# A gated-MLP kernel with a hand-written planner: own PSUM tiles for the block products of v, measured durations in the planner, and another order of its steps

## The chip, the cores and the metric

The kernel runs on one core of one Trainium2 chip. The metric is the device time of one execution in microseconds (us), the median of several runs. The engines are named as in the profile: PE (TensorE, matmuls), DVE (VectorE), ACT (ScalarE), POOL (GpSimd) and SP (the sync engine, which here issues the DMAs).

## What is computed

Two parts follow one another: a block attention whose blocks are 64 tokens long, and a gated MLP on its result with a spatial mixing by `w_sg`. All of it is float32.

```python
def _attn_ref(q, k, v):                       # (batch, heads, seq, head_dim) = (8, 8, 576, 64), chunk = 64
    ...
    scores = scale * np.matmul(q_c, k_c.transpose(0, 1, 2, 4, 3))      # within each chunk of 64 tokens
    attn = np.exp(scores - np.max(scores, axis=-1, keepdims=True))
    attn = attn / (np.sum(attn, axis=-1, keepdims=True) + 1e-09)
    return np.matmul(attn, v_c).reshape(B, H, S, D)

def _moe_ref(x, w_in, g_ln, w_sg, b_sg, w_out):   # x (8, 576, 512), w_in (512, 1024), w_out (512, 512)
    h = gelu_tanh(x @ w_in)
    u, v = h[..., :512], h[..., 512:]
    v_n = (v - mean(v)) / np.sqrt(var(v) + 1e-06) * g_ln
    v_s = np.einsum('ts,bsd->btd', w_sg, v_n) + b_sg[None, :, None]
    return x + (u * v_s) @ w_out
```

## The kernel before

The work is cut by batch entry ("block" b, 0 to 7). Each block passes four stages: v (the right half of `x @ w_in`, then gelu and the layer norm), u (the left half), s (the mixing by `w_sg`, times u) and o (`@ w_out`, plus x, and the stores). Attention runs in tiles of 128 tokens: scores (S, 64x64 matmuls and a softmax), a transpose (T) and the product with the attention's values (O, 64x64 matmuls, copied out of PSUM into `xh`, `xl`, `xf`). The attention of a later block is laid between the MLP steps of an earlier one.

Every float32 operand is split into a high and a low part (`split`), and a product takes three matmuls (low by high, high by low, high by high). From block `FAST` = 2 on, the products of v, u and o are done by a seven-product scheme for 2x2 blocks: `product` (L1209) with number 1 to 7. Sums of weight blocks that it needs are made once by `w_sums` on POOL, kept in DRAM and loaded into the tile `wx` ahead of each stage (`next_extra`); sums of x blocks are made for each block by `x_sums` on POOL and split by ACT and DVE into `tx`.

PSUM is one pool of four tiles of two banks each (`ps_m`, `[P, 2, 512]` float32, program name `pm` in the trace). `v_fast` takes one such tile for two accumulators, `o["a"]` in the first bank and `o["b"]` in the second: product 1 into a, a copied out by ACT, product 5 into b, b copied out by ACT, product 6 into a, a copied out, product 3 into b, b added up by DVE, product 7 into a, and so on. A further tile `c` is taken in its last step. `u_fast`, by contrast, takes a tile of its own for each of its accumulators a, b and c, with both banks of each in use.

The order of all instructions is made when the program is built. Each call of an engine is recorded (`Recorder`, `Plan.add`) with its dependencies; `cells` and `masks` say which part of a tile an operand covers, for PSUM by the bank (2048 bytes). `Op.price` gives each instruction a duration and a lag, `Plan.due` a due time, and `Plan.run` simulates the engines and picks for each the ready instruction with the earliest due time. PE goes through its instructions in the order of the program but may look up to `AHEAD` = 10 us of work further. `EARLY` moves the due times of named steps, `LATE` = 60 ns is added to every wait between engines. `emit` (L230) then issues all instructions in the order of the simulated start times (L253, the one line that nearly all rows of the trace carry), and the framework below adds the semaphores, from the order in which it sees the instructions. Each engine executes its queue strictly in that order, so an instruction at the head that is not ready holds up all behind it.

The order that the planner starts from is written by hand. `START` (L48) lists the steps of blocks 0 and 1, the weight conversion and the first attention tiles: L and W, w (load, begin, end of the v half of `w_in`), X and x (the u half), Y (`w_out`), G and g (`w_sg`), A and B (loads of q/k and of the attention's values), S, T, O, P, Q (attention), v, u, s, o with block and step, V and Z (`w_sums` of u and of v), E (`odd_diff`) and J (`x_sums`). SP issues the loads of START in exactly this order up to the step `V0`. Blocks 2 to 7 run in the loop at its end; `SLOTS` says behind which unit of a block which attention steps are put (one list for odd blocks, one for even ones), and `SUMS` behind which units of block 2 the `w_sums` of o are put.

Of the kernel before, what the change touches and what calls it, by code (L numbers as in the profile page):

```python
# [25 lines left out]
P = 128  # L26
# [22 lines left out]
A0 L0 B0 A1 L1 L2 L3 B1 A2 A3 S0 W0 T0 S1 W1 S2 w0 w1 T1 W2 O0 O1 W3 w2 T2 S3 M0 w3 v00 O2 A4 T3 X0 O3 G0 S4 v01 A8 T4  # L49
O4 B8 x0 X1 v02 X2 x1 v03 X3 U1 v04 U0 x2 g0 g1 x3 g2 g3 P5 g4 F0 u02 u03 s00 T5 F1 T6 P7 s01 s02 Q5 T7 T8 s03 Q7 v10  # L50
v11 Y0 v12 v13 Y4 Y2 Y1 Y3 u10 u11 s10 u13 Y5 s11 Y6 Y7 u12 A10 V0 P9 B10 A11 V1 s12 o01 V2 S13 A12 T9 T10 o02 V3 P11 A15 T13 o03 s13 o00 Q9 B11 T11 T12 O13 B12 Z0 Z1 o10 Z2 o11 Z3 Q11 B15 P14 A17
E2 o12 o13 J0 J1 J2
"""

SUMS = {8: "o0", 9: "o1", 10: "o2", 11: "o3"}
# [12 lines left out]
    1: "0:T0 1:S4 1:T1 3:S23 4:T4 8:O01 8:T2 9:O4 10:T3 11:O23 11:S56",  # L68
    0: "0:T5 1:T6 2:S78 9:O56 9:T7 10:T8 12:O78 12:S9A",
# [7 lines left out]
FAST = 2  # L77
ORDER = "u0 u1 u2 u3 u4 s0 s1 s2 s3 o0 o1 o2 o3"
# [9 lines left out]
EARLY = {'K*': 0, 'X*': -8, 's03': 1, 'Y0': -2, 'P7': 3, 'v04': -4, 'X0': -1, 'w3': -1, 'W*': -1, 'g4': 5, 'Y7': -2}  # L88
# [4 lines left out]
LATE, DMA_LATE = 60, 3000  # L93
# [15 lines left out]
@functools.cache  # L109
def masks(ap, offset, width, psum):  # L110
    (step, n), *free = ap
    row, at = offset // step, offset % step
    idx = np.array([at])
    for st, c in free:
        idx = (idx[:, None] + st * np.arange(c)[None, :]).ravel()
    unit = 2048 if psum else 128 if step * width > 256 else 4
    mask = 0
    for i in np.unique(idx * width // unit):
        mask |= 1 << int(i)
    if psum:  # L120
        return (mask, 0, 0, 0)
    return tuple(mask if row < 32 * (q + 1) and row + n > 32 * q else 0 for q in range(4))
# [10 lines left out]
class Op:  # L133
# [11 lines left out]
    def price(self):  # L145

        n = max(a.free_size() for a in self.outs[:1] + self.ins[:2])
        psum = any(a.space == PSUM for a in self.outs + self.ins)
        if self.engine == "tensor":
            x = self.ins[-1]  # L150
            n = self.outs[0].free_size()
            if x.dtype == F32R:
                return (5.9 if n < 400 else 4.6) + 0.447 * n, 160
            if x.dtype == BF16:
                return 4.6 + 0.42 * n, 160
            if self.ins[0].ap[0][1] == D:
                self.quarter = True
                return 34, 160
            return (118 if self.method == "transpose" else 1.83 * n + 10), 160
        if self.method == "dma_start" and self.engine == "gpsimd":  # L160
            return 1200, DMA_LATE + self.ins[0].size() / 100
        if self.engine == "sync":
            row = self.ins[0].ap[-1][1]
            return (420 if row >= P else 620), DMA_LATE + self.ins[0].size() / row / 16 * (9 + 0.16 * row)
        wide = [a for a in self.ins if a.free_size() > 1]
        copies = self.method in ("tensor_copy", "tensor_scalar") and n > 1
        if self.engine == "gpsimd":
            self.waits = self.method == "tensor_tensor"
            self.locks = self.waits and n > 8
        if self.engine == "vector":  # L170
            if self.method == "memset":
                return 600, 80
            self.locks = self.waits = not psum and (len(wide) > 1 or copies)
            one = len(self.ins) == 1 and not psum and self.method in ("tensor_copy", "tensor_scalar")
            return 75 + (0.53 if one else 1.04) * n, 80
        if self.engine == "scalar":
            return 100 + 0.82 * n + (100 if len(self.outs) > 1 else 0), 100
        return (600 if "pow" in str(self.kwargs.get("op")) else 200 + 1.8 * n), 42
# [10 lines left out]
class Plan:  # L189
# [84 lines left out]
    def run(self, users, after, at):  # L274
# [41 lines left out]
        for _ in range(len(ops)):  # L316
# [39 lines left out]
            if e == "tensor" and op.quarter != mode:  # L356
                mode = op.quarter
                cost += 150
            if e == "scalar" and op.table not in (0, table):
                table = op.table  # L360
                cost += 1200
# [53 lines left out]
def block_attention_gated_mlp(ctx: ExitStack, tc: tile.TileContext, qkv, w_in, w_out, w_sg, g_ln, b_sg, out):  # L415
# [177 lines left out]
    def w_sums(kind, step):  # L593
# [5 lines left out]
        def whole(i, j):  # L599
            r = new()  # L600
# [7 lines left out]
        def store(n):  # L608
            before, nc.early = nc.early, 1000 * EARLY.get("K*", 0)
            for a, c in zip(kept[kind], extras()):  # L610
                nc.sync.dma_start(out=blocks_of(a, 3)[:, n].bitcast(F32), in_=c[:, n].bitcast(F32))
            nc.early = before

        if step == 0:
            kept[kind] = [spare.tile([P, 3 * 4 * P], F32R, name=f"kept_{kind}_{i}") for i in range(2)]
            sums["11"], sums["21"] = whole(0, 0), whole(1, 0)
            s3 = new()
            pick("c").tensor_tensor(s3, sums["11"], sums["21"], op=ALU.subtract)
            split_to([a[:, 1] for a in extras()], s3)
            store(1)  # L620
        elif step == 1:
            r = whole(1, 1)
            pick("c").tensor_tensor(sums["21"], sums["21"], r, op=ALU.add)
            pick("c").tensor_tensor(sums["11"], sums["21"], sums["11"], op=ALU.subtract)
            split_to([a[:, 0] for a in extras()], sums["11"])
            store(0)
        elif step == 2:
            r = whole(0, 1)
            pick("c").tensor_tensor(r, r, sums["11"], op=ALU.subtract)
            split_to([a[:, 2] for a in extras()], r)  # L630
            store(2)
        else:
            split_to(block(1, 0), sums["21"])

    wx, kept = {}, {}
    NEXT = {"v": "u", "u": "o", "o": "v"}

    def next_extra(kind, b, n):

        kind = NEXT[kind]  # L640
        if (b == FAST and kind == "o") or (b == B - 1 and kind == "v"):
            return
# [220 lines left out]
    def keep_tile(place, src):  # L863
        (b, c), (b1, c1) = place
        if b == b1 and c and (c != 4 or b < FAST):
# [31 lines left out]
    def keep(b, c, src, tiles=0):  # L897
# [21 lines left out]
        if c > 4 and b >= FAST:  # L919
# [69 lines left out]
    def v_unit(b, m):  # L989
# [7 lines left out]
        for kt in range(KT):  # L997
            ab = [(h_in, l_in)[k][:, kt, tok] for k in (1, 0, 0)]
            cs = win_h, win_l, win_h
            if b < FAST or kt < 2:  # L1000
# [421 lines left out]
```

## Time and profile before

| | before |
|---|---|
| median of 3 runs | 527.72 us (526.66 to 528.29) |
| the profiled execution | 529.48 us, of which the span from first to last instruction is 527.7 us |
| busy: PE, DVE, ACT, POOL | 483.1, 419.2, 346.2, 139.4 us |
| mean granted TensorE clock | 0.987 |
| blocks 0 and 1 with all preparation | until about 172 us |
| blocks 2 to 7 | about 58 to 65 us each, the last one without attention beside it |

The table of stages and the groups of instructions show where PE is idle and what ended the idle time; the timelines show the instructions of one engine in order, with the idle time before an instruction and its releaser in square brackets. In the names, `pm<-wx,tx` is a matmul that reads `wx` and `tx` and writes a PSUM tile. In stage v the names stand as `wx,tx`, `win_l,tx`, `wx,xh` (256 columns), in stage u as `tx,wx`, `tx,win_l` (288 columns), in stage o as `gl,wout` and the like.

### The profile page before, as it was taken

What the parts mean: (1) busy time and instruction counts of PE and PEld (TensorE: products, weight loads), DVE (VectorE), ACT (ScalarE), POOL (GpSimd) and SP (SyncE); (2) the same over time, 40 slices, a digit from 0 to 9 for tenths busy, and PEclk for the clock granted to TensorE, in tenths of its full rate; (3) what the DMA queues carried; (4) which work ended last, traced back from release to release, by engine and by line L of the source; (5) the groups of instructions that cost most, each with busy time, mean ns of one, the idle gap of its engine ahead of it and who ended that gap; (6) DMA issues with size and microseconds to landing.
All of it is one profiled execution on the core that took longest, in us unless ns stands there. A gap on an engine that the chain in (4) does not pass through costs nothing.

```text
span 527.7 us, 13136 instructions
## 1 busy us (share of the span) xinstructions
PE 483.1 (92%) x5305; PEld 449.5 (85%) x5310; DVE 419.2 (79%) x741; ACT 346.2 (66%) x629; POOL 139.4 (26%) x129
## 2 busy tenths in 40 slices
PE   3999999999978989999898899989997898998995
PEld 2568997999867988999898899989897888998995
DVE  7979998998947896897969696979757599685565
ACT  4887899436664897658973798549884398534420
POOL 0113100830354728133311421151301522130100
PEclk9999999999989999999999999999997999999998
DMA  8884102038627812487544643288520745055303
GB/s 331 289 240 132 41 1 81 1 107 240 219 69 231 260 52 87 138 264 234 164 114 135 193 165 101 87 233 256 162 97 5 233 133 141 20 155 176 121 0 91
DMA packets 80828, 76.53 MB, mean 145 GB/s; under 512 B 47100, under 2 KB 60672, under 8 KB 80768
## 3 DMA queue, kind: packets, MB, share of 16 engines
q1 hardware_dynamic: 80768, 75.69, 46.6%
q8 instruction: 42, 0.69, 0.5%
q14 instruction: 18, 0.15, 0.1%
HBM read 61.51 MB, written 14.16 MB: 143 GB/s over the span
## 4 chain that ended last, share of the span: by engine, by line
PE 31%; DVE 29%; ACT 22%; DMA 6%; issue 5%; POOL 4%; SPq 1%; DVEq 0%; POOLq 0%; ACTq 0%
PE pm L253 31%; ACT ptT L253 6%; DVE nmax L253 4%; DVE u L253 4%; DVE sm L253 3%; ACT u L253 2%; DVE xl L253 2%; DVE gl L253 2%; DMA out_dram<-ot 2%; DVE pt L253 2%; ACT L253 2%; ACT xf L253 2%; DVE st L253 2%; DVE wout L253 2%; DVE v L253 2%
## 5 line engine op out<-in xcount | busy, mean ns | idle before, releaser
L253 PE MATMUL pm<-wsg,v 128*128 128x288 f32 x768 | 109.3, 298 | 3.0 <-DVE ut L253 2.9
L253 PEld LDWEIGHTS pm<-wsg,v 128*128 128x128 f32 x768 | 103.7, 189 | 4.5 <-PE pm L253 2.2
L253 ACT COPY ptT<-blocks 32x256 f32<-32x256 f32 (+1 forms) x140 | 62.5, 447 | 12.5 <-DVE blocks L253 10.1
L253 POOL TENSOR_TENSOR sm<-sm,neg_half 128x1 f32<-128x1 f32 x36 | 30.1, 838 | 122.3 <-DVE sm L253 110.8
L253 PE MATMUL pm<-gh,wout 128*128 128x288 f32 x272 | 56.0, 303 | 2.1 <-DVE xl L253 1.1
L253 DVE TENSOR_TENSOR u<-pm,u 128x576 f32<-128x576 f32 (+1 forms) x50 | 36.0, 726 | 25.8 <-PE pm L253 25.2
L253 PEld LDWEIGHTS pm<-gh,wout 128*128 128x128 f32 x272 | 43.6, 192 | 3.5 <-issue 1.3
L253 POOL TENSOR_TENSOR pt<-pt,nmax 128x512 f32<-128x512 f32 x27 | 30.4, 1140 | 50.5 <-DVE nmax L253 44.9
L253 PE MATMUL pm<-gl,wout 128*128 128x288 f32 x136 | 36.4, 306 | 5.6 <-DVE gl L253 5.5
L253 ACT ACT_TABLE_LOAD x30 | 38.5, 1283 | 4.5 <-DVE pt L253 3.3
L253 ACT CAST gh<-u 128x576 fp32r<-128x576 f32 x32 | 21.4, 671 | 25.2 <-DVE u L253 25.1
L253 POOL TENSOR_TENSOR xs<-xf 128x576 f32<-128x576 f32 x12 | 18.2, 1513 | 60.8 <-ACT xf L253 41.1
L253 POOL TENSOR_TENSOR xs<-xf,xs 128x576 f32<-128x576 f32 x12 | 19.0, 1582 | 51.4 <-DVE tx L253 36.0
L253 DVE TENSOR_TENSOR gl<-u,gh 128x576 fp32r<-128x576 f32 x32 | 26.5, 833 | 6.5 <-ACT gh L253 6.1
L253 ACT CAST tx<-xs 128x576 fp32r<-128x576 f32 x24 | 16.1, 674 | 21.8 <-POOL xs L253 15.2
L253 PEld LDWEIGHTS pm<-gl,wout 128*128 128x128 f32 x136 | 24.3, 192 | 6.9 <-DVE gl L253 6.9
L253 DVE TENSOR_TENSOR ot<-pm,xf 128x576 f32<-128x576 f32 x32 | 23.8, 750 | 7.0 <-PE pm L253 4.9
L253 DVE TENSOR_TENSOR tx<-xs,tx 128x576 fp32r<-128x576 f32 x24 | 20.6, 865 | 10.9 <-ACT tx L253 10.7
L253 PE MATMUL pm<-xh,win_l 128*128 128x288 f32 x112 | 28.3, 299 | 0.0
L253 PE MATMUL pm<-qk 64*64 64x64 f32 x992 | 20.8, 228 | 8.0 <-DMA qk<-qkv 6.9
L253 PE MATMUL pm<-xh,win_h 128*128 128x288 f32 x112 | 28.0, 296 | 0.0
L253 PE MATMUL pm<-xl,win_h 128*128 128x288 f32 x112 | 28.0, 296 | 0.0
(185 smaller groups left out, 1329.4 us busy)
## 6 DMA issues: line engine op xcount, KB each, us to landing
qk<-qkv SPq DMA_DIRECT2D x31, 512.0 KB, 4.8
wx<-kept_u SPq DMA_DIRECT2D x36, 256.0 KB, 3.3
out_dram<-ot SPq DMA_DIRECT2D x31, 256.0 KB, 4.0
wx<-kept_v SPq DMA_DIRECT2D x30, 256.0 KB, 4.5
wx<-kept_o SPq DMA_DIRECT2D x30, 256.0 KB, 3.3
av<-qkv SPq DMA_DIRECT2D x116, 64.0 KB, 2.6
wsg<-w_in SPq DMA_DIRECT2D x4, 512.0 KB, 8.8
wout<-w_in SPq DMA_DIRECT2D x4, 512.0 KB, 6.8
```

What stands on the lines that cost most here:

```text
L253: getattr(getattr(self.nc, op.engine), op.method)(*op.args, **op.kwargs)
```

## The change

Each accumulator of `v_fast` gets a PSUM tile of its own. For the planner, a PSUM tile is now one cell, whichever bank is used. `Op.price` is rewritten with other durations and lags for nearly every kind of instruction, `LATE` goes from 60 to 0, and the change of PE between 64-row and 128-row matmuls costs 90 or 253 ns in the simulation where it cost 150. `START` is reordered, `SLOTS` has a list for each block, `SUMS` moves two of the sums of o, and `EARLY` grows from 11 to 71 entries. The sums of v's weights (`w_sums("v", ...)`) are computed in three steps in place of four, with block sums computed again where they were held before: 13 additions or subtractions on POOL where there were 8. The last store of the program is one addition over both halves, with two DMAs (one from SP, one from ACT's queue) where there were two additions and four DMAs from SP. `FAST_V` equals `FAST`, so that every test with it gives what it gave.

```diff
 START = """
-A0 L0 B0 A1 L1 L2 L3 B1 A2 A3 S0 W0 T0 S1 W1 S2 w0 w1 T1 W2 O0 O1 W3 w2 T2 S3 M0 w3 v00 O2 A4 T3 X0 O3 G0 S4 v01 A8 T4
...
-v11 Y0 v12 v13 Y4 Y2 Y1 Y3 u10 u11 s10 u13 Y5 s11 Y6 Y7 u12 A10 V0 P9 B10 A11 V1 s12 o01 V2 S13 A12 T9 T10 o02 V3 P11 A15 T13 o03 s13 o00 Q9 B11 T11 T12 O13 B12 Z0 Z1 o10 Z2 o11 Z3 Q11 B15 P14 A17
-E2 o12 o13 J0 J1 J2
+L0 A1 S0 L2 L1 A0 S1 L3 B1 A2 W3 W1 A3 T0 S2 W2 B0 T1 W0 w0 O1 A4 w2 X0 O0 T2 M0 w1 S3 w3 v00 O2 T3 S4 G0 O3 v01 T4
...
+Q7 v10 v12 v11 Y0 Y1 Y3 v13 Y5 u10 Y7 u11 Y2 Y6 s10 A11 u12 u13 s11 V0 P9 V1 T9 S13 s12 B10 A10 o01 V2 T10 o02 A12
+P11 T13 o03 s13 o00 V3 Q9 T11 B11 Z0 T12 O13 B15 Z1 o10 A17 o11 A15 B12 Z2 o13 Q11 E2 o12 J0 J2 P14 J1
 """
-SUMS = {8: "o0", 9: "o1", 10: "o2", 11: "o3"}
+SUMS = {(2, 8): "o0", (2, 9): "o1 o2", (2, 11): "o3"}
 SLOTS = {
-    1: "0:T0 1:S4 1:T1 3:S23 4:T4 8:O01 8:T2 9:O4 10:T3 11:O23 11:S56",
-    0: "0:T5 1:T6 2:S78 9:O56 9:T7 10:T8 12:O78 12:S9A",
+    2: "10:S9A 0:T5 10:O56 10:T8 12:O78 1:S78 4:T6 8:T7",
+    3: "9:T4 2:T1 2:S4 10:O4 1:T0 12:O23 3:S23 9:O01 8:T2 9:T3 9:S56",
+    4: "10:S9A 10:O56 8:T7 9:T8 2:T6 2:S78 1:T5 12:O78",
+    5: "9:T4 2:T1 10:O4 1:T0 3:S23 9:O01 2:S4 12:O23 8:T2 9:T3 9:S56",
+    6: "12:S9A 2:S78 8:T8 12:O78 10:O56 0:T5 6:T7 1:T6",
 }
-LATE, DMA_LATE = 60, 3000
+LATE, DMA_LATE = 0, 3000
@@ masks
-    unit = 2048 if psum else 128 if step * width > 256 else 4
+    if psum:
+        return (1, 0, 0, 0)
+    unit = 128 if step * width > 256 else 4
@@ Op.price (PE; GpSimd; ScalarE)
-                return (5.9 if n < 400 else 4.6) + 0.447 * n, 160
+                return 2.5 + 0.45 * n, 190
...
-        return (600 if "pow" in str(self.kwargs.get("op")) else 200 + 1.8 * n), 42
+            if "pow" in str(self.kwargs.get("op")):
+                return 870, 42
+            return (300 + 0.5 * n if not self.waits else 100 + (1.76 if self.kwargs["op"] == ALU.mult else 2.27) * n), 42
...
-            return 100 + 0.82 * n + (100 if len(self.outs) > 1 else 0), 100
+        slow = 120 * (len(outs) > 1) + 90 * (len(ins) > 1)
+        return (80 if psum else 100) + (0.8 if psum else 0.825) * n + max(slow, 105 * part), 100
@@ w_sums, kind "v" (new)
+            if step == 0:
+                r, r2 = whole(0, 0), whole(1, 0)
+                add(r, r2, ALU.subtract)
+                keep_sum(1, r, r2)
+            elif step == 1:
+                r, r2 = whole(1, 0), whole(1, 1)
+                add(r, r2)
+                whole(0, 0, r2)
+                add(r, r2, ALU.subtract)
+                whole(0, 1, r2)
+                add(r2, r, ALU.subtract)
+                keep_sum(0, r)
+                keep_sum(2, r2)
+            else:
+                r, r2 = whole(1, 0), whole(1, 1)
+                add(r, r2)
+                split_to(block(1, 0), r)
@@ v_fast
-            ab = ps_m.tile([P, 2, 512], F32, name="pm")
-            o["a"], o["b"] = ab[:, 0], ab[:, 1]
+            o["a"], o["b"] = (ps_m.tile([P, 2, 512], F32, name="pm")[:, 0] for _ in range(2))
@@ o_fast, the last step of block 7
-            for e in range(2):
-                es = slice(e, e + 1)
-                o_part(d, ot, ot, es)
-                o_store(b, 1, 0, ot, es)
+            o_store(b, 1, 0, o_part(d, ot, ot), last=nc.scalar)
```

## Rows read from the trace of the kernel before

**Rows 1.** The page, part 1: busy time, share of the span, instructions by engine.
```profile
PE 483.1 (92%) x5305; PEld 449.5 (85%) x5310; DVE 419.2 (79%) x741; ACT 346.2 (66%) x629; POOL 139.4 (26%) x129
```
**Rows 2.** Busy time by stretch: length, engines' busy (x instructions), granted clock, DMA share, GB/s.
```profile
0.00:40.00 40.00, 29.49 (x361) 20.07 (x364) 33.41 (x72) 28.63 (x63) 4.58 (x10) 1.00 0.84 288
40.00:140.00 100.00, 98.88 (x1041) 91.21 (x1042) 92.90 (x179) 69.94 (x127) 25.08 (x22) 1.00 0.33 97
140.00:172.00 32.00, 26.21 (x352) 23.29 (x351) 21.41 (x34) 18.45 (x45) 14.83 (x13) 0.95 0.55 161
```
**Rows 3.** PE groups of stage v: xcount | busy us, mean ns | idle before, releasers.
```profile
L253 PE MATMUL pm<-wx,tx 128*128 128x256 f32 x144 | 21.4, 289 | 4.7 <-ACT u L253 2.7 <-DVE u L253 2.0
L253 PE MATMUL pm<-win_l,tx 128*128 128x256 f32 x48 | 14.0, 291 | 1.8 <-ACT u L253 1.4 <-DVE u L253 0.5
L253 PE MATMUL pm<-wx,xh 128*128 128x256 f32 x48 | 10.4, 289 | 1.5 <-ACT u L253 1.5
```
**Rows 4.** Timeline of PE in stage v of block 7: start, duration, [idle before <-releaser].
```profile
474.12 0.52 PE L253 MATMUL pm<-wx,tx 128*128 128x256 f32 x3
475.31 1.35 PE L253 MATMUL pm<-wx,tx 128*128 128x256 f32 x9 [0.68 <-ACT u L253]
```
**Rows 5.** Timeline of ACT in the same stretch.
```profile
474.67 0.58 ACT L253 COPY u<-pm 128x512 f32<-128x512 f32 x1 [2.55 <-PE pm L253]
```
**Rows 6.** PE groups of stage u, columns as in rows 3.
```profile
L253 PE MATMUL pm<-tx,wx 128*128 128x288 f32 x144 | 21.7, 298 | 2.0 <-ACT ut L253 2.0
...
L253 PE MATMUL pm<-tx,win_l 128*128 128x288 f32 x48 | 14.7, 306 | 0.9 <-DVE ut L253 0.9
```
**Rows 7.** Timeline of PE where block 5 goes from s to o.
```profile
393.24 0.70 PE L253 MATMUL pm<-wsg,z 128*128 128x288 f32 x4
...
402.46 0.61 PE L253 MATMUL pm<-gl,wout 128*128 128x288 f32 x1 [0.88 <-DVE gl L253]
```
**Rows 8.** Timeline of DVE there.
```profile
396.35 1.21 DVE L253 TENSOR_REDUCE nmax<-pm 128x16 f32<-128x1024 f32 x1
...
398.57 0.75 DVE L253 TENSOR_TENSOR u<-pm,u 128x576 f32<-128x576 f32 x1
```
**Rows 9.** Two stretches at the lower clock, and block 5 from s to o; columns as rows 2.
```profile
148.97:152.38 3.41, 3.41 (x23) 2.76 (x22) 1.60 (x4) 1.78 (x5) 0.00 (x0) 0.50 0.09 20
401.55:408.38 6.83, 5.95 (x25) 5.92 (x25) 4.86 (x8) 3.17 (x5) 0.00 (x0) 0.50 0.00 0
390.00:416.00 26.00, 22.85 (x141) 21.39 (x141) 20.65 (x33) 10.83 (x20) 5.58 (x5) 0.87 0.39 128
```
**Rows 10.** PE waiting for gl in stage o: the group (as rows 3).
```profile
L253 PE MATMUL pm<-gl,wout 128*128 128x288 f32 x136 | 36.4, 306 | 5.6 <-DVE gl L253 5.5
```
**Rows 11.** Timeline of PE at the end of blocks 0 and 1.
```profile
148.76 0.70 PE L253 MATMUL pm<-gl,wout 128*128 128x288 f32 x2 [2.07 <-DVE gl L253]
...
157.01 0.51 PE L253 MATMUL pm<-qk 64*64 64x64 f32 x19 [1.17 <-ACT xf_lows L253]
```
**Rows 12.** Groups of ACT and POOL with durations that the planner prices.
```profile
L253 ACT COPY ptT<-blocks 32x256 f32<-32x256 f32 x112 | 45.2, 404 | 2.1
...
L253 POOL TENSOR_TENSOR sm<-sm,neg_half 128x1 f32<-128x1 f32 x36 | 30.1, 838 | 122.3 <-DVE sm L253 110.8 <-ACT z L253 6.2 <-DMA av<-qkv 3.3
...
L253 POOL TENSOR_TENSOR r<-win_h,win_l 128x512 f32<-128x512 f32 x8 | 10.7, 1337 | 2.8 <-DVE wx L253 1.5 <-DVE v L253 1.0 <-ACT ptT L253 0.3
```
**Rows 13.** Timeline of POOL: the first sum of x for block 2.
```profile
170.29 1.43 POOL L253 TENSOR_TENSOR xs<-xf 128x576 f32<-128x576 f32 x1 [5.62 <-DVE x_diff L253]
```
**Rows 14.** Timeline of PE and ACT at the start: the first scores, the first weight.
```profile
4.31 1.13 PE L253 MATMUL pm<-qk 64*64 64x64 f32 x32 [4.31 <-DMA qk<-qkv]
...
5.53 0.66 ACT L253 ACTIVATE wsg<-wsg 128x512 f32<-128x512 f32 x1 [2.80 <-DMA wsg<-w_in]
```
**Rows 15.** Timeline at the end: the last additions (DVE), the last store's issue (SP).
```profile
522.89 0.82 DVE L253 TENSOR_TENSOR ot<-pm,ot 128x288 f32<-128x288 f32 x2
...
524.74 0.42 SPq L253 DMA_DIRECT2D out_dram<-ot  x1
```

More of the change, by code (lines that the diff above doesn't have):

```diff
@@ L77 @@
 FAST = 2
+FAST_V = 2
 ORDER = "u0 u1 u2 u3 u4 s0 s1 s2 s3 o0 o1 o2 o3"
@@ L606, in split_to, with store, keep_sum @@
             split(place[0], place[1], src, nc.scalar, nc.vector)
-        def store(n):
+        def store(n, place):
             before, nc.early = nc.early, 1000 * EARLY.get("K*", 0)
-            for a, c in zip(kept[kind], extras()):
-                nc.sync.dma_start(out=blocks_of(a, 3)[:, n].bitcast(F32), in_=c[:, n].bitcast(F32))
+            for a, c in zip(kept[kind], place):
+                nc.sync.dma_start(out=blocks_of(a, 3)[:, n].bitcast(F32), in_=c.bitcast(F32))
             nc.early = before
+        def keep_sum(n, src, hi=None):
+            place = [a[:, n] for a in extras()]
+            if kind == "v" and FAST_V > FAST:
+                place = [(new() if hi is None else hi).bitcast(F32R), src.bitcast(F32R)]
+            split_to(place, src)
+            store(n, place)
@@ new lines, in add @@
+        def add(a, c, op=ALU.add, to=None):
+            pick("c").tensor_tensor(a if to is None else to, a, c, op=op)
+        if kind == "v":
+            if step == 0:
+                kept[kind] = [spare.tile([P, 3 * 4 * P], F32R, name=f"kept_{kind}_{i}") for i in range(2)]
+                r, r2 = whole(0, 0), whole(1, 0)
[14 more added lines that the diff above has]
+                split_to(block(1, 0), r)
+            return
@@ L638, in next_extra @@
     def next_extra(kind, b, n):
-        kind = NEXT[kind]
-        if (b == FAST and kind == "o") or (b == B - 1 and kind == "v"):
+        if kind == "o":
+            b, kind = b + 1, "v" if b + 1 >= FAST_V else "u"
+        else:
+            kind = "u" if kind == "v" else "o"
+        if b == B or kind not in kept or (b == FAST and kind == "o"):
             return
@@ L1255, in o_store @@
             dst = out[b, 2 * i : 2 * i + 2, :, to].rearrange("e p s -> p e s")
-            nc.sync.dma_start(out=dst[:, es], in_=ot[:, es, of])
+            (last if of is rest[1] and last else nc.sync).dma_start(out=dst, in_=ot[:, :, of])
     def o_fast(b, step):
@@ L1314, in att_slots @@
         slots = [[] for _ in range(n)]
-        for step in SLOTS[b % 2].split() if b + 1 < B else ():
+        for step in SLOTS.get(b, "").split():
             i, what = step.split(":")
@@ L1360, in block_attention_gated_mlp @@
         units = [] if b % 2 else [(v_unit, 4)]
-        units += [(v_fast, k) for k in range(4)]
+        units += [(v_fast if b >= FAST_V else v_unit, k) for k in range(4)]
         units += [(f, int(i)) for x in ORDER.split() for f, i in [({"u": u_fast, "s": s_unit, "o": o_fast}[x[0]], x[1])]]
```

94 lines of the change are left out of this document (46 added, 48 removed).

## The prediction

> **What bounds the kernel now.** I read the page first. PE is busy for 483.1 of 527.7 us [rows 1], so it is the bound, and no edit changes what it computes. All that the change can win is the 44.6 us in which PE is idle, and what PE loses while its clock is granted at half. I therefore asked for the busy time by stretch: of 44.6 us, 10.5 fall in the first 40 us, 1.1 in the next 100, and 5.8 between 140 and 172, where blocks 0 and 1 end [rows 2]; 4.8 us are the tail from the last additions on [rows 15]; the other 22.4 lie in blocks 2 to 7. To see what these are I took the groups of PE's matmuls by form. Stage v has 8.0 us in three groups (4.7, 1.8, 1.5), ended by ACT or DVE working on `u`, that is on the accumulators [rows 3]. Matmuls that wait for `gl` in stage o have 5.6 us over the whole run [rows 10]. Stage u has 2.9 us [rows 6]. The granted clock stood at 0.50, the lower of its two levels (1.2 in place of 2.4 GHz), for two stretches of 3.41 and 6.83 us [rows 9]; there PE does half of what it would, so they cost about 1.7 and 3.4 us. That is a bound on the gain: nothing here is worth more than these items.
>
> **The accumulators of v.** The timeline of block 7 shows what the waits are. Product 6 writes accumulator a. Its first three matmuls run at 474.12; the fourth stands until 475.31, with 0.68 us of idle time put down to ACT [rows 4]. In between, at 474.67, ACT copies an accumulator out, and it starts just when the third of those matmuls ended [rows 5]. That copy reads b, which product 5 has just finished. So ACT waited for a matmul into the other bank, and then PE waited for ACT: both orders are false, and the only thing that a and b share is the PSUM tile. The planner takes banks for independent and puts the copy in the middle of product 6; whatever sets the semaphores takes the tile as one. The first half of the edit (a tile each) removes the dependency, the second half (one cell a tile) makes the planner see what the semaphores do.
>
> The gain is bounded by 8.0 us if nothing else is late [rows 3]. The bound from the other side is stage u, which has the same pattern with tiles of its own and keeps 2.9 us in six blocks [rows 6], because a itself must be copied out before product 6 may write it; that leaves 8.0 - 2.9 = 5.1. What would be late next in v is just this copy: 0.58 us of ACT [rows 5] beside the twelve matmuls of product 5, nine of which take 1.35 us [rows 4], so it has cover unless ACT is held up. I take the middle, **6.5 us**.
>
> The Trainium skill ("PSUM — Partial Sum Buffer", Summary: rules for kernel authors) says to read PSUM while matmuls run from a different bank, and to guard by bank and quadrant. By that rule a and b in two banks of one tile were already apart and the waits must have another cause, which would make the split worth 0 and the time some 523; this is the first rival. The trace speaks against it, since ACT started on the end of a matmul into the other bank.
>
> The price of the edit is PSUM: in steps 0 and 1 of `v_fast` two of four tiles are held where one was. Tile b comes free at the end of step 1, before c is taken, so the peak of two is not raised. I cost it at nothing, because score groups in these steps are one to a block. If that cover fails it is the slow rival below.
>
> **The durations and the order.** The worst place outside v is block 5 from s to o. PE ends stage s at about 393.9, and the o matmuls that wait for `gl` resume at 402.46 [rows 7]. DVE is why: the multiplication by u of the last row of s, ready at 393.9, starts at 398.57, behind attention work such as a reduction of 1.21 us [rows 8]. PE is idle for 3.15 of the 26 us there, and the half clock of 6.83 us follows directly [rows 9]. The same wait ends blocks 0 and 1, with 2.07 us at 148.76, then 3.41 us at half clock [rows 9, 11]. Both are orders of a queue that came out wrong, and the planner's durations may explain how: by its formulas it takes the copies of 32 partitions of `ptT` for 310 ns where the row says 404, with 112 of them, the power on POOL for 600 where the row says 838, an addition on POOL for 1122 where the row says 1337 [rows 12]. A planner that is short in all of these believes that DVE will have attention work sooner than it has. The new durations are 415, 870 and 1262. Also `SLOTS` moves the products of tiles 2 and 3 in blocks 3 and 5 behind the last step of s, and scores 5 and 6 two steps ahead, so that less of that work comes due at the transition.
>
> I count block 5's 3.15 us as gone by two thirds and the clock stretch behind it as gone: 2.1 + 3.4 = **5.5 us**; bounds 0 and 6.6 us. Another 0.9 us for the remaining waits on `gl` in block 3 (5.6 in all, of which block 5's and the 2.07 us are part [rows 10, 11]). But an order in which every queue is dealt anew makes waits of its own. Blocks 2 to 7 have 22.4 - 8.0 = 14.4 us of such idle time under the old order, 2.4 us a block. I charge one block's worth, **2.4 us**, for new ones; the bounds are 0 and twice that.
>
> **Blocks 0 and 1.** Three things meet here. (a) SP loads the first weight ahead of the first q and k. Before, the scores start at 4.31 and the first weight is there at 5.53 [rows 14]; exchanged, the weight's conversion starts about a microsecond sooner and the scores as much later. In the first 40 us DVE is busy for 33.4 [rows 2], and both go through DVE, so I cost it at 0; bounds -1.2 and +1.2. (b) `w_sums` of v makes five additions more on POOL, 5 x 1.34 = 6.7 us [rows 12], ahead of the sums of x for block 2. Before the first of these POOL sat idle for 5.62 us [rows 13], and in 140 to 172 it works 14.8 of 32 us [rows 2]; that is the cover, and I cost the additions at 0. If the cover is gone they cost up to 6.7. What is gained by them is that two of the four temporary buffers are no longer held over three steps. The Trainium skill ("SBUF — State Buffer", Who interferes with whom) has it that a DVE instruction with two SBUF inputs and a POOL instruction that reads SBUF exclude each other. By it the five additions would take as much from DVE, at worst 6.7 us; no row here isolates that. DVE has 10.6 us free in this stretch [rows 2]. (c) The new order may close the 5.8 us of idle time and the 1.7 us of clock there [rows 2, 9], or open more. The wait at 157.01 is one of PE on ACT [rows 11], so it is not only DVE. Bounds: -7.5 to +6.7. I take -1.5, a fifth of what is there, as the step order after s of block 1 is nearly the old one.
>
> **The tail.** The last additions start at 522.89 and take 0.82 us as two halves; the last store is issued at 524.74 [rows 15]. As one, the addition takes about 0.75 and both stores are issued at some 523.7, side by side on two queues. The transfer is then twice as long for each; I take back half of the 1.0 us: **-0.5 us**, bounds 0 and -1.0.
>
> **The sum.** 529.5 (the profiled execution: its span of 527.7 and 1.8 around it) - 6.5 - 5.5 - 0.9 + 2.4 - 1.5 - 0.5 = 517.0. The median of the runs lies 1.8 us under the profiled one, so the sum is 515.2 against the median. Since all terms but the first lean on a schedule that I have not seen, I round it up to 516.0.
>
> **The rivals.** First, v's waits are not removed but moved, or were never false: PE reaches s sooner and waits there for the layer norm, or the copy of a is late each time. For it speaks that stage u keeps a third of such waits with its own tiles [rows 6]; against it, the ACT copy that started on a foreign matmul [rows 4, 5]. Time: 516.0 + 6.5 = 522.5. Second, the new order repairs nothing net: only v and the tail count, 527.7 - 6.5 - 0.5 = 520.7, and with the full price of new waits (4.8) 525.5. Third, better than forecast: with durations near the truth the planner closes the whole of 140 to 172 (another 6.0) and some 3 us more of the 14.4 in blocks 2 to 7: 516.0 - 9 = 507. Fourth, slower: PSUM runs short. In each of blocks 2 to 7 the start of v needs two tiles while the last o accumulator is still read; in three blocks a tile for `v_unit` comes on top, and in three a score group within the first two steps: 12 places. A wait of PE for a PSUM tile's reader is of the size of the one at 157.01, 1.17 us [rows 11], so 12 x 1.17 = 14.0, and 516.0 + 14.0 = 530.0. It is slower than before from about 0.98 us a place. Against it: b is released early, and the planner knows the four tiles and can lay other matmuls in.
>
> **How the numbers follow.** Forecast 0.49; moved waits 0.13; order repairs nothing 0.15; better 0.13; PSUM short 0.10. The forecast's own range goes from 510 to 522. To leave out no more than 2 in 10, I cut off half of the slow case, a third of the better one, and the edges of the rest: 506 to 527. A measurement of this kernel can tell 0.3%, that is 1.6 us, from no change. The slow case gives slower 0.10, and a few of the second rival's outcomes fall within 0.3% or above: faster 0.82, same 0.07, slower 0.11.
>
> **What would show it.** Right: no wait of PE on ACT's or DVE's `u` in the groups of stage v beyond 3 us in sum; the multiplication after s3 of block 5 within a microsecond of the last s matmul; no half clock near 400 us; the last store issued within 1 us of the start of the last addition. Wrong: waits of 0.7 us kept in v under another releaser (first rival); PE waiting for readers of PSUM tiles at the start of v (fourth); POOL late with `xs` before block 2, or a second half-clock stretch in blocks 0 and 1.

## The result and the profile after

| | before | after |
|---|---|---|
| median | 527.43 us (526.66 to 528.29, 4 runs) | 504.35 us (504.03 to 505.13, 4 runs) |
| ratio after to before | | 0.9564, 95% interval 0.9545 to 0.9583 |
| span of the profiled execution | 527.7 us | 503.3 us |
| mean granted clock in it | 0.987 | 0.999 |

The change makes the kernel 23 us faster. The forecast was 516.0 with a range of 506 to 527, so the sign was right and the size was not: 23 us where 11.7 were forecast, 1.7 us outside the range.

The page of after, part 1, answers [rows 1]:

```profile
PE 474.7 (94%) x5310; PEld 444.0 (88%) x5310; DVE 419.0 (83%) x740; ACT 343.7 (68%) x627; POOL 143.5 (29%) x134
```

PE still does the same matmuls, but in 8.4 us less of busy time, and its idle time fell from 44.6 to 28.6 us. Of the 8.4 us some 4.7 are an accident of the execution that was profiled (an estimate): the two stretches at the lower level in [rows 9] hold 3.41 + 5.95 us of PE's busy time, half of which would do at the higher one, and the profile of after has a granted clock of 1.00 in every stretch below. The busy time by stretch of after, columns as in [rows 2]:

```profile
0.00:40.00 40.00, 26.81 (x345) 17.48 (x346) 31.38 (x67) 24.71 (x57) 3.80 (x10) 1.00 0.73 263
40.00:140.00 100.00, 98.95 (x1032) 90.09 (x1032) 91.89 (x177) 71.11 (x128) 25.27 (x23) 1.00 0.34 101
140.00:172.00 32.00, 27.96 (x381) 25.34 (x380) 24.34 (x40) 21.91 (x51) 23.96 (x19) 1.00 0.63 195
172.00:503.30 331.30, 320.96 (x3557) 311.08 (x3556) 271.39 (x457) 226.01 (x394) 90.45 (x84) 1.00 0.50 150
```

and the last of these stretches in the kernel before:

```profile
172.00:527.70 355.70, 328.55 (x3557) 314.94 (x3555) 271.52 (x459) 229.21 (x397) 94.88 (x84) 0.99 0.46 141
```

Blocks 0 and 1 gave nothing: the first 40 us have 13.2 us of idle time instead of 10.5, the stretch from 140 to 172 has 4.0 instead of 5.8. Everything came from blocks 2 to 7: 355.7 us became 331.3 with the same number of PE's matmuls in the trace, 3557. The idle time there went from 27.2 to 10.3 us.

Where it went is told by PE's groups of after, columns as in [rows 3]. The first three answer [rows 3], the next two [rows 6], the sixth [rows 10]:

```profile
L264 PE MATMUL pm<-wx,tx 128*128 128x256 f32 x144 | 20.0, 282 | 0.2 <-ACT u L264 0.2
L264 PE MATMUL pm<-win_l,tx 128*128 128x256 f32 x48 | 13.6, 284 | 0.0
L264 PE MATMUL pm<-wx,xh 128*128 128x256 f32 x48 | 9.7, 283 | 0.3 <-DMA wx<-kept_v 0.3
...
L264 PE MATMUL pm<-tx,wx 128*128 128x288 f32 x144 | 21.4, 297 | 0.0
L264 PE MATMUL pm<-tx,win_l 128*128 128x288 f32 x48 | 14.4, 300 | 0.0
L264 PE MATMUL pm<-gl,wout 128*128 128x288 f32 x136 | 35.7, 299 | 1.0 <-DVE gl L264 1.0
L264 PE MATMUL pm<-wsg,v 128*128 128x288 f32 x768 | 110.2, 297 | 0.0
```

The last is the main group of stage s, which in the kernel before reads

```profile
L253 PE MATMUL pm<-wsg,v 128*128 128x288 f32 x768 | 109.3, 298 | 3.0 <-DVE ut L253 2.9
```

The waits of v went from 8.0 to 0.5 us, as forecast or better. But those of u went too (2.9 to 0), those of s (3.0 to 0), and those on `gl` (5.6 to 1.0). The forecast had charged 2.4 us for new waits there.

### The profile page after: what moved, and what is told of

The parts are those of the page before. It is cut to its first block, busy times and chain, and to the rows that moved or that the text cites. A ratio compares the mean times of both kernels' runs of the same rounds, so it can differ in the third digit from the quotient of the medians.

```text
span 503.3 us, 13159 instructions
## 1 busy us (share of the span) xinstructions
PE 474.7 (94%) x5310; PEld 444.0 (88%) x5310; DVE 419.0 (83%) x740; ACT 343.7 (68%) x627; POOL 143.5 (29%) x134
## 4 chain that ended last, share of the span: by engine, by line
PE 65%; ACT 16%; DVE 12%; DMA 3%; issue 2%; POOL 1%; SPq 0%; ACTq 0%; DVEq 0%; POOLq 0%
PE pm L264 63%; ACT ptT L264 5%; ACT xf L264 2%; PE banks L264 2%; DVE nmax L264 2%; DVE xl L264 2%; ACT xh L264 2%; ACT gh L264 1%; DMA out_dram<-ot 1%; ACT pt L264 1%; DVE ot L264 1%; DVE wsg L264 1%; ACT L264 1%; DMA wx<-kept_v 1%; DVE gl L264 1%
## 5 line engine op out<-in xcount | busy, mean ns | idle before, releaser
L264 POOL TENSOR_TENSOR sm<-sm,neg_half 128x1 f32<-128x1 f32 x36 | 28.0, 781 | 114.5 <-DVE sm L264 87.1
L264 POOL TENSOR_TENSOR pt<-pt,nmax 128x512 f32<-128x512 f32 x27 | 29.1, 1093 | 47.1 <-DVE nmax L264 42.7
L264 DVE TENSOR_TENSOR gl<-u,gh 128x576 fp32r<-128x576 f32 x32 | 25.3, 792 | 10.5 <-ACT gh L264 10.5
L264 PE MATMUL pm<-win_l,xh 128*128 128x256 f32 (+1 forms) x80 | 26.8, 335 | 1.5 <-ACT hs L264 1.5
L264 PE MATMUL pm<-win_h,xl 128*128 128x256 f32 (+1 forms) x80 | 26.5, 331 | 0.4 <-DVE xl L264 0.4
L264 DVE TENSOR_TENSOR xl<-pm,xh 128x256 fp32r<-128x256 f32 (+2 forms) x37 | 17.4, 490 | 11.2 <-ACT xf L264 10.0
```

Of the source, the lines that this page charges most:

```text
L264: getattr(getattr(self.nc, op.engine), op.method)(*op.args, **op.kwargs)
```

## The experiments

**Three parts, each alone and in pairs.** I cut the change into the tiles (own tiles for v's accumulators and one planner cell a tile), the durations (`price`, the change of PE's mode, `LATE` = 0) and the order (`START`, `SLOTS`, `SUMS`, `EARLY`, the sums of v, the tail). With before and after, six kernels complete the set. The edits are the parts of the diff shown ahead of the prediction, applied to the kernel before or taken out of the kernel after. The two halves of the tiles, the tile itself and the planner's cell, were not run apart.

b_tiles, the tiles alone:

```diff
-    unit = 2048 if psum else 128 if step * width > 256 else 4
+    if psum:
+        return (1, 0, 0, 0)
+    unit = 128 if step * width > 256 else 4
...
-            ab = ps_m.tile([P, 2, 512], F32, name="pm")
-            o["a"], o["b"] = ab[:, 0], ab[:, 1]
+            o["a"], o["b"] = (ps_m.tile([P, 2, 512], F32, name="pm")[:, 0] for _ in range(2))
```

> The kernel before, with a PSUM tile for each accumulator of v and one planner cell for each PSUM tile; old durations, old order. Theory 1 (the false waits of v are the main thing, each worth its idle time and about 0.16 us of lost overlap at the restart): 15 stalls, 8.1 + 2.4 us, so 517 us, and no more than 1 us of waits left in v. Rival (the waits only move to s, or the order makes the gain): 523 to 528 us.

b_prices, the durations alone (two lines stand for the whole of `price`):

```diff
-LATE, DMA_LATE = 60, 3000
+LATE, DMA_LATE = 0, 3000
...
-                return (5.9 if n < 400 else 4.6) + 0.447 * n, 160
+                return 2.5 + 0.45 * n, 190
```

> The kernel before, with the new durations and no added wait in the planner alone; shared tile of v, old order. Theory 2 (wrong durations made the queues of DVE and ACT come out in a bad order, so they hold the 14 us outside v): 515 to 520 us, with the waits of v still there at about 8 us. Rival (the hand-written order and the due times, fitted to the new durations, hold that gain): 524 to 532 us, since the old entries of EARLY were fitted to the old durations.

b_tiles_prices, both of these:

> The kernel before, with the tiles of v, the cells and the new durations, but the old order of steps, blocks and sums. If the parts add up by theories 1 and 2: 507 to 512 us. If the order carries the gain outside v: 516 to 522 us.

a_order, the kernel after without either:

> The kernel after, with v's accumulators in one tile again, cells by the bank, and the old durations: the new order (steps, attention blocks, sums, due times, tail) alone. Theories 1 and 2: it was fitted to the new durations and is worth nothing or less without them, 524 to 534 us. Rival (the order carries the gain outside v): 512 to 518 us.

a_oldprices, tiles and order:

```diff
-LATE, DMA_LATE = 0, 3000
+LATE, DMA_LATE = 60, 3000
...
-                return 2.5 + 0.45 * n, 190
+                return (5.9 if n < 400 else 4.6) + 0.447 * n, 160
```

> The kernel after, planned with the old durations and the old added wait; tiles, cells, steps, attention blocks, sums and due times as in after. Theory 3 (the durations are what makes a planned order hold on the chip): 515 to 528 us, with the new idle time in s, u and o. Rival (the hand-written order and the due times carry it): at most 510 us.

a_shared, durations and order:

> The kernel after with v's accumulators in one tile and PSUM cells by the bank, planned anew with the new durations. If the false waits simply add: 513 to 518 us. If, as before, dealing the queues anew costs more than the part itself: up to 528 us.

Measured, with the ratio to the kernel before in the same job:

| tiles | durations | order | kernel | median us | ratio (95%) |
|---|---|---|---|---|---|
| - | - | - | before | 527.43 | 1 |
| x | - | - | b_tiles | 527.87 | 1.0001 (0.998 to 1.0022) |
| - | x | - | b_prices | 529.76 | 1.0044 (1.0026 to 1.0063) |
| - | - | x | a_order | 537.59 | 1.0190 (1.0162 to 1.0217) |
| x | x | - | b_tiles_prices | 517.47 | 0.9819 (0.9791 to 0.9847) |
| x | - | x | a_oldprices | 522.38 | 0.9905 (0.988 to 0.9931) |
| - | x | x | a_shared | 531.00 | 1.0073 (1.0049 to 1.0098) |
| x | x | x | after | 504.35 | 0.9564 (0.9545 to 0.9583) |

No part gains anything alone; the order loses 1.9% and the durations 0.4%. The tiles are worth nothing on top of before, 1.0044 - 0.9819 = 2.3% on top of the durations, 2.9% on top of the order, and 1.0073 - 0.9564 = 5.1%, some 27 us, on top of both. So theories 1 and 2, under which each part has a value that adds up, are wrong. So is "the order carries it": b_tiles_prices lies in the range that this reading gave (516 to 522), but a_order, for which it gave 512 to 518, is the slowest of the eight. a_shared lies 3 us above the wider of its two ranges. What each part is worth depends on which of the others are there.

**The tiles at a fixed order.** In b_tiles most of the waits of v are gone all the same (1.4 us are left of 8.0); its groups, as in [rows 3]:

```profile
L253 PE MATMUL pm<-wx,tx 128*128 128x256 f32 x144 | 20.4, 287 | 0.6 <-ACT u L253 0.3 <-DVE tx L253 0.2
L253 PE MATMUL pm<-win_l,tx 128*128 128x256 f32 x48 | 13.9, 289 | 0.8 <-ACT ptT L253 0.8
L253 PE MATMUL pm<-wx,xh 128*128 128x256 f32 x48 | 9.6, 282 | 0.0
```

But every queue has been dealt anew, so this doesn't say what the tiles cost or give. Two kernels do: the order of all instructions is written into them as a list, taken from the planner of before or after, and only the tiles differ.

```diff
+ORDERED = ( ... )   # the order of the 5982 (before) or 5984 (after) recorded instructions, packed
...
-        at = None
-        for _ in range(3):
-            at = self.run(users, after, at)
+        order = np.frombuffer(zlib.decompress(base64.b64decode(ORDERED)), np.uint16)
...
-            for k in sorted(range(len(ops)), key=lambda k: (at[k], k)):
+            for k in order.tolist():
```

> The kernel after with every instruction in its own order, and only the two accumulators of v put back into one PSUM tile. Theory: some 15 false waits come back, at 0.83 us each, 513 to 518 us, with 8 to 11 us of waits in v. Rival (an order in which these waits do not matter): at most 507 us.

a_fixed_shared: 514.97 us, ratio 0.9765 (0.974 to 0.9789), 10.6 us slower than after in the very same order. The waits are back:

```profile
L387 PE MATMUL pm<-wx,tx 128*128 128x256 f32 x144 | 21.4, 287 | 5.1 <-DVE u L387 4.5 <-ACT u L387 0.6
L387 PE MATMUL pm<-win_l,tx 128*128 128x256 f32 x48 | 13.7, 286 | 1.4 <-ACT u L387 1.4
L387 PE MATMUL pm<-wx,xh 128*128 128x256 f32 x48 | 10.1, 289 | 2.0 <-ACT u L387 2.0
```

These are 8.5 us in 11 stalls, and a twelfth of 0.7 us, also on ACT's `u`, stands before `win_h,tx`: 9.2 us, against 0.5 in after. A stall costs more than its idle time, since the matmuls no longer overlap across it: in [rows 4] the third matmul starts at 474.12 + 0.52 - 0.28 = 474.36 and the fourth at 475.31, 0.95 us apart where 0.13 is the pace of the nine that follow, so 0.82 is lost and 0.68 is shown as idle. By that estimate 8.7 + 12 x 0.14 = 10.4 of the 10.6 us. The rows agree: the three groups are busy for 45.2 us where after has 43.3, 1.9 us more with the same matmuls. Theory 1 holds here, in the order that was planned for tiles of their own.

> The kernel before with every instruction of every engine in exactly the order that its planner gave it, and only the two accumulators of v in PSUM tiles of their own. Theory (the false waits are real and cost PE their idle time and the lost overlap; the earlier run with the tiles gained nothing because the planner dealt all queues anew): 517 to 520 us, waits of v under 2 us. Rival (they only move elsewhere): 525 to 528 us with longer waits in s and u.

b_fixed_tiles: 530.68 us, ratio 1.0070 (1.0037 to 1.0102). In the order of before the tiles gain nothing and rather cost 0.4 to 1.0%, though its three groups of v have only 1.3 us of waits left; both ranges were missed. The profile is of the fastest of its eight executions, 527.63 us, which is the time of before; the others took 528.1 to 535.2 us, on the whole the longer the lower their mean granted clock was (0.994 down to 0.976), and no trace of them was kept. In the profile other waits took the place of v's. PE and, in the last two lines, DVE and ACT around the start of v in blocks 2 and 3:

```profile
175.38 0.81 PE L376 MATMUL pm<-qk 64*64 64x64 f32 x40 [2.27 <-ACT hs L376]
...
183.08 0.37 PE L376 MATMUL pm<-xh,win_l 128*128 128x288 f32 x1 [2.20 <-DVE pt L376]
...
237.97 0.36 PE L376 MATMUL pm<-win_l,xh 128*128 128x256 f32 x1 [2.27 <-DVE pt L376]
...
181.65 1.29 DVE L376 TENSOR_TENSOR pt<-pm,nmax 128x512 f32<-128x512 f32 x2
...
173.43 1.28 ACT L376 ACT_TABLE_LOAD   x1
```

Each is the first matmul into a new PSUM tile, and each waits for the reader of an older one: the gelu of `v_unit`, or the softmax reading scores (it ends at 182.94, PE starts at 183.08). That the older tile is what they wait for is inferred from this timing. These three are 6.7 us, as much as v's groups lost (8.0 to 1.3); in the first, ACT loads a table for 1.28 us ahead of the gelu, so more than half of that wait is the table. This is the fourth rival of the prediction, PSUM running short, with fewer places and a price of 2.2 instead of 1.17 us each. An order that is planned with the tiles in view avoids most of it: in after one such wait is left (1.45 us on `hs` in block 2).

**Plan and chip.** Each kernel's planner ends its simulation with a time for PE's last instruction. Beside it the end of the last matmul in the trace:

| kernel | plan us | trace us | distance |
|---|---|---|---|
| before | 491.7 | 521.7 | 30.0 |
| b_prices | 488.1 | 522.6 | 34.5 |
| a_order | 496.9 | 531.2 | 34.3 |
| a_shared | 486.5 | 524.7 | 38.2 |
| b_tiles | 497.7 | 519.2 | 21.5 |
| b_tiles_prices | 486.4 | 509.1 | 22.7 |
| a_oldprices | 497.9 | 515.0 | 17.1 |
| after | 480.4 | 498.1 | 17.7 |

The first four share v's tile and plan by banks: the chip runs 30 to 38 us behind the plan. The last four have the tiles: 17 to 23 us. So in these eight kernels the tiles change how well the plan holds, while durations and order change how short it is. The tiles alone don't make a plan hold: a_oldprices_late0, below, has them and is 41 us behind. A shorter plan that doesn't hold gains nothing (b_prices, a_shared), and a plan that holds better but has become longer gains nothing either (b_tiles: 6 us longer; that the planner now counts PSUM as scarcer is the likely reason, and not shown).

**The durations and the margin.** The prediction had not costed `LATE` at all. Two kernels split the durations of after from the margin of 60 ns that the planner added to each wait:

```diff
 (a_late60)
-LATE, DMA_LATE = 0, 3000
+LATE, DMA_LATE = 60, 3000
 (a_oldprices_late0: old durations)
 LATE, DMA_LATE = 0, 3000
```

> The kernel after with its own durations, and only the 60 ns put back that the planner adds to every wait between engines. Theory 4 (this margin, and not the measured durations, is what lengthened the plan: the planner's own end of PE's work is 499.2 us here, 480.4 in after and 497.9 with all old durations): 518 to 524 us, like the kernel after with all old durations (522.4). Rival (the measured durations make the plan hold): at most 510 us.

> The kernel after with the old durations, but without the 60 ns of margin; the other half of the pair. Theory 4: 505 to 512 us, the durations are worth little. Rival: 515 to 524 us, the durations carry it.

| | margin 60 | margin 0 |
|---|---|---|
| old durations | 522.38 (a_oldprices) | 536.60, ratio 1.0172 (a_oldprices_late0) |
| new durations | 516.24, ratio 0.9789 (a_late60) | 504.35 (after) |

Neither theory held. With the margin the new durations gain 6 us; without it they gain 32. With the new durations, dropping the margin gains 12 us; with the old ones it loses 14. The plan of a_oldprices_late0 ends at 489.6 and the chip's last matmul at 530.7, 41 us behind: the worst of all. Its PE waits in many places, for these three up to 2.5 us at a time:

```profile
PE pm L257 <- ACT ptT L257: 5.5, 7, 1.8
PE pm L257 <- DVE ot L257: 4.9, 3, 2.5
PE pm L257 <- DVE u L257: 3.2, 4, 1.4
```

(columns: us in total, times, longest). This is what one would see if the margin covered for wrong durations, so that it can go only with measured ones. It is not shown that nothing else is at work: `START`, `SLOTS` and `EARLY` of after belong to the new durations at a margin of 0, and no run fits them anew for the other three cells of the table. Whether the size of the margin or merely another deal of the queues costs the time was asked with 20 ns:

> The kernel after with a margin of 20 ns in place of 0 on every wait between engines in the planner; its own end of PE's work is 487.4 us. Theory (a third of the margin costs a third of the 11.9 us that 60 ns cost): 507 to 509 us. Rival (any other value deals the queues anew against due times that were fitted at 0, and costs much the same as 60): 511 to 517 us.

511.74 us, ratio 0.9704 (0.9676 to 0.9732): 20 ns cost 7.4 of the 11.9 us. That lies in the rival's range: the loss doesn't grow in step with the margin. That the due times no longer fit is the rival's reason for it, and not shown by this run; the planner's own end moves by about as much as the chip, 7.0 us (480.4 to 487.4).

**The hand-written pieces.** Each put back alone into after:

```diff
 (a_oldslots)
-    3: "9:T4 2:T1 2:S4 10:O4 1:T0 12:O23 3:S23 9:O01 8:T2 9:T3 9:S56",
...
+    1: "0:T0 1:S4 1:T1 3:S23 4:T4 8:O01 8:T2 9:O4 10:T3 11:O23 11:S56",
+    0: "0:T5 1:T6 2:S78 9:O56 9:T7 10:T8 12:O78 12:S9A",
 (a_oldearly: the 11 old entries of EARLY)
 (a_oldstart: the old START and w_sums)
```

> The kernel after with the two old lists that place attention steps beside the blocks. Theory (the attention blocks placed late in s kept DVE from the work that o waits for): waits on gl and ot come back in blocks 3 and 5, 508 to 514 us. Rival (the planner sorts by due times, so the lists matter little): at most 506 us.

> The kernel after with the 11 old entries of the due-time table. It moves the planner's own end of PE's work from 480.4 to 484.9 us. Theory (a shorter plan is kept by the chip, one to one, once the tiles are apart): 507 to 511 us. Rival (the table is fitted to the planner alone, and the chip does not follow): 503 to 506 us.

> The kernel after with the old list of steps for blocks 0 and 1 and the old sums of v's weights (eight additions on POOL in place of thirteen, the first q and k ahead of the first weight). The planner's own end of PE's work is 482.8 us in place of 480.4. Theory (blocks 0 and 1 gave nothing; in after the first 40 us hold 2.7 us more idle time and block 2's v starts no earlier): 503 to 508 us. Rival (the new list and sums carry a part of the gain like the other hand-written pieces): 510 to 516 us.

a_oldslots 515.16 us (0.9766, 0.9751 to 0.9781), a_oldearly 512.47 (0.9723, 0.9697 to 0.9748), a_oldstart 508.94 (0.9657, 0.9627 to 0.9688): 10.8, 8.1 and 4.6 us slower than after. The first two lie 1 to 2 us above the ranges of their theories, the third between its two ranges. They don't add up either (the whole order is worth 13 us on top of tiles and durations). And the chip doesn't follow the plan one to one: for a_oldearly and a_oldstart the planner's end moved by 4.5 and 2.4 us, the chip's time by about twice that. For the lists of attention steps the mechanism of the prediction is there. DVE in a_oldslots where block 5 goes from s to o, and PE behind it:

```profile
389.74 1.21 DVE L261 TENSOR_REDUCE nmax<-pm 128x16 f32<-128x1024 f32 x1
390.99 1.29 DVE L261 TENSOR_TENSOR pt<-pm,nmax 128x512 f32<-128x512 f32 x2
392.19 0.75 DVE L261 TENSOR_TENSOR u<-pm,u 128x576 f32<-128x576 f32 x1
...
394.15 0.40 PE L261 MATMUL pm<-gl,wout 128*128 128x288 f32 x1 [1.36 <-DVE gl L261]
```

It is [rows 8] again: softmax work for scores 5 and 6 ahead of the multiplication that o waits for. Over the whole run the waits on `gl` are 2.7 us there and those of `wsg,v` 1.8. In after the same place reads

```profile
379.90 0.69 PE L264 MATMUL pm<-wsg,z 128*128 128x288 f32 x4
...
382.84 0.75 DVE L264 TENSOR_TENSOR u<-pm,u 128x576 f32<-128x576 f32 x1
...
386.57 0.40 PE L264 MATMUL pm<-gl,wout 128*128 128x288 f32 x1 [0.49 <-DVE gl L264]
```

with no softmax in between. The multiplication still comes 2.25 us after the last matmul of s (4.6 in [rows 7, 8]), but PE has matmuls to fill that.

**A better version, and how far the plan can be trusted.** If a shorter plan now holds, more can be had by making it shorter. I changed the table of due times at random and kept what shortened the planner's own end, three times independently; nothing else differs from after.

> The kernel after with a table of due times that was changed until the planner's own end of PE's work fell by 1.3 us, from 480.4 to 479.1; nothing else differs. Theory (the chip keeps a shorter plan one to one now): 502.5 to 503.5 us. Rival (at this size the plan tells nothing; the distance of plan and chip differs by several us between orders): 503 to 511 us, more likely above 504.

> As the first fitted table, but another table, found independently; the planner's own end of PE's work is 479.3 us in place of after's 480.4. Theory (a shorter plan is kept by the chip): 500 to 504 us. Rival (the 3 us of the first table were luck): 504 to 511 us.

> A third independent table, the planner's own end of PE's work 479.35 us. Theory: 500 to 504 us. Rival: 504 to 511 us.

| kernel | plan us | median us | ratio to before (95%) |
|---|---|---|---|
| after | 480.4 | 504.35 | 0.9564 (0.9545 to 0.9583) |
| a_early_fit | 479.1 | 501.31 | 0.9505 (0.9479 to 0.9531) |
| a_early_fit2 | 479.3 | 503.96 | 0.9539 (0.9518 to 0.9560) |
| a_early_fit3 | 479.35 | 506.40 | 0.9563 (0.9512 to 0.9613) |

The first table beats both kernels, at 501.31 us. Its stretch from block 2 on has 7.1 us of idle time, where after has 10.3:

```profile
172.00:499.40 327.40, 320.33 (x3569) 312.49 (x3567) 271.19 (x460) 226.13 (x394) 94.11 (x85) 1.00 0.51 153
```

But three plans that end within 0.3 us of each other have medians up to 5 us apart, and that distance is itself uncertain: the four executions of a_early_fit3 took 501.49 and 506.05 to 506.76 us, so one of them was as fast as a_early_fit, and the intervals of the two overlap. The theory's range was met by the second table, missed by the first (it was better) and by the third. At steps of 1 us the plan doesn't order the kernels; a fitted order has to be timed, and more than a few times.

## Why the prediction was wrong

**The false waits of v: right in mechanism, short in size.** I took 6.5 us. At the fixed order of after it is 10.6; at the fixed order of before it is nothing, as three waits for PSUM tiles (6.7 us) eat it up, which I had costed at nothing. So the term has no size apart from the order. Two more steps were off. I bounded the gain by the idle time, 8.0 us; the lost overlap at each stall was left out. And I took stage u's 2.9 us as what own tiles must keep; in after u has 0, so that was no floor but another wrong order. The first rival, that the banks were apart already, is out: a_fixed_shared shows that the waits come and go with the tile alone, in the same order (9.2 us against 0.5). The rule of the Trainium skill ("PSUM — Partial Sum Buffer", Summary: rules for kernel authors) is about which bank may be read while matmuls run, and not about what this program's semaphores hold apart.

**The durations and the order: the wrong sign of one term.** The step that failed is "I charge one block's worth, 2.4 us, for new ones". It treated the 14.4 us of idle time outside v in blocks 2 to 7 as something that any order has, took 3.0 us off (2.1 in block 5, 0.9 for the other waits on `gl`) and put 2.4 on. In after 5.8 us are left of it (10.3, less 4.0 of the tail and 0.5 of v): 8.6 us went where I had 0.6. Together with the 4.1 us that v was short this is about the size of the miss. Over the whole run the groups above lose 2.9 + 3.0 + 4.6 = 10.5 us. What took them away can be read from the same groups in the eight kernels (idle time of PE in us, one profiled execution each; v, u and `gl` as in [rows 3, 6, 10], s is `wsg,v`):

| kernel | tiles | durations | order | v | u | s | `gl` | all idle |
|---|---|---|---|---|---|---|---|---|
| before | - | - | - | 8.0 | 2.9 | 3.0 | 5.6 | 44.6 |
| b_tiles | x | - | - | 1.4 | 2.8 | 4.8 | 1.5 | 42.4 |
| b_prices | - | x | - | 8.6 | 2.8 | 4.2 | 2.1 | 44.2 |
| a_order | - | - | x | 11.4 | 2.7 | 1.3 | 0.4 | 46.4 |
| b_tiles_prices | x | x | - | 1.7 | 1.9 | 2.6 | 4.3 | 35.6 |
| a_oldprices | x | - | x | 1.3 | 3.7 | 0.0 | 1.0 | 38.6 |
| a_shared | - | x | x | 8.1 | 2.2 | 0.1 | 0.6 | 45.4 |
| after | x | x | x | 0.5 | 0.0 | 0.0 | 1.0 | 28.6 |

The waits of v go with the tile. Those of s and on `gl` are lowest in the four kernels with the new order, also in a_shared, whose plan is 38 us off. Those of u go only where all three parts are together. But without the tiles all idle time stays at 44 to 46 us whatever leaves s and `gl`: it comes back in other places. This fits parts that don't add up. I had looked for what a better order does at the worst place (5.5 us) and not asked how far the chip ran behind the plan as a whole. Nor did the prediction add the parts as they act: it summed tiles, durations and order as if independent. Why the idle time moves instead of going away while the tile is shared was not traced further.

**The margin was not costed.** `LATE` from 60 to 0 was named in the change and left out of the working. In after it is worth 11.9 us (7.4 already at 20 ns), with the old durations it costs 14.

**The half clock was over-counted.** I took 3.4 us for one stretch at the lower level [rows 9], out of one execution. Among the 53 executions of the kernel before that ran beside the experiments, the seven with a mean granted clock of 0.998 or more took 526.1 to 528.5 us, the four with 0.989 or less 528.7 to 530.3: 2.6 us between their means, for all such stretches together. The profiled one, 0.987, was among the worst. Of 23 us between the medians the clock explains 1 or 2 by this estimate, and it isn't the order that removes it for good: the fastest run of after had 0.988.

**Blocks 0 and 1.** (a) The exchange of the first loads: the first weight's conversion starts at 4.27 instead of 5.53 and the scores at 5.71 instead of 4.31, about as worked out, but the transpose behind them waits and the first 40 us lose 2.7 us where I had 0 (bounds 1.2). The exchange isn't shown to be the cause: a_oldstart, with the old list, has 13.9 us of idle time in the first 40 where after has 13.2 and before 10.5. The rows of after:

```profile
5.71 1.13 PE L264 MATMUL pm<-qk 64*64 64x64 f32 x32 [5.71 <-DMA qk<-qkv]
...
13.45 0.90 PE L264 MATMUL banks<-ident,first_pts 128*128 128x128 f32 x3 [2.91 <-DVE first_pts L264]
```

(b) The five more additions on POOL don't delay the sums of x (169.75 where [rows 13] have 170.29), but the last block of weights comes late after them, and PE waits 2.6 us for it, where I had 0 and a bound of 6.7:

```profile
166.11 1.27 POOL L264 TENSOR_TENSOR r<-r 128x512 f32<-128x512 f32 x1
...
169.00 0.50 PE L264 MATMUL pm<-win_h,xodd 128*128 128x512 f32 x1 [2.64 <-ACT win_h L264]
```

I had asked only who stands behind them on POOL, not who waits for their result. On the whole the stretch from 140 to 172 is no worse for it: 4.0 us of idle time, and 4.1 in a_oldstart, which has no such wait. a_oldstart is still 4.6 us slower, with 3.0 us of waits in v. What its list does for blocks 2 to 7 I did not trace further.

**The tail: right.** From the last matmul to the end of the span it was 6.0 us before and is 5.2 after, 0.8 us less; I had taken 0.5. The last addition and the store on ACT's queue:

```profile
499.31 0.76 DVE L264 TENSOR_TENSOR ot<-pm,ot 128x576 f32<-128x576 f32 x1
...
500.10 0.47 ACTq L264 DMA_DIRECT2D out_dram<-ot  x1
```

**The signs.** Three of the four signs of being right came true: 0.5 us of waits in v, no half clock near 400 us, the last store issued 0.8 us after the start of the last addition. The multiplication after s3 of block 5 did not come within a microsecond (2.25 us). None of the four looks at the waits in u and s, where the size was missed.

**The rivals.** The third came nearest (507), by luck: I had laid 6 of its 9 us into 140 to 172, where 1.8 came. The mechanism of the fourth is what b_fixed_tiles shows, with the tiles in the old order. That its times are close (530.0 and 530.7) is chance: the rival added 14.0 us of waits to all the other gains, and b_fixed_tiles has 6.7 us of them and none of those gains.

## What to carry to other kernels

Where a planner orders the work, first compare its own end with the chip's: a distance of 30 us with 45 us of idle time says that the model is wrong somewhere; here a shorter plan paid only when that was mended. Make the model see what the semaphores see (here the tile, not the bank), measure the durations, and only then take the safety margin out. Parts of such a change could not be priced one by one, and a part tested alone may look worthless or harmful: hold the order fixed to see what a part does, and put parts back into the whole to see what they are worth there.

## What was not expected of the hardware

A stall of PE costs about 0.14 us more than the idle time that the profile shows for it, as the overlap of its 0.28 us matmuls is lost (0.82 against 0.68 in [rows 4]; 1.9 us more of busy time for 11 stalls in a_fixed_shared). And the stretches at the lower clock level differ between executions of one program: mean granted clock 0.987 to 0.999 for the same kernel before, with 525.7 to 530.3 us, and 0.976 to 0.994 for b_fixed_tiles, with 527.6 to 535.2.
